# Agent attention and a three-way max network in one kernel: the last group stored as four output tiles, and new places for operations of the head

## The chip, the cores and the metric

The kernel runs on one NeuronCore of one Trainium2 chip. The metric is the device time of one execution in microseconds (us). Four executions were timed: 451.83, 451.85, 452.03 and 456.93 us, so the median is 451.94 us. One further execution was recorded by the hardware profiler, and all rows in this text come from that one.

## The reference

```python
def sm(a, b):                                  # softmax of scaled scores
    s = scale * (a @ b.transpose(0, 2, 1))
    e = np.exp(s - s.max(-1, keepdims=True))
    return e / (e.sum(-1, keepdims=True) + 1e-09)
agent_v = sm(agents, k) @ v                    # 49 agents gather from 12544 keys
x = sm(q, agents) @ agent_v                    # each query reads the 49 agents
h = np.maximum(np.maximum(x @ w1, x @ w2), x @ w3)
out = h @ w_out
```

There are 4 batches of 12544 rows and 128 columns, 49 agents, and weights of 128 x 768 (three) and 768 x 128. Inputs and output are float32.

## The kernel before, in words

**Folding.** Queries meet the weights only through 49 agent rows. So per batch a small matrix `G` is made from `agent_v` times the weights, in three parts: w2 - w1 (columns from `C21`), w3 - w1 (columns from `C31`; for one of the six blocks of 128, `f = FI = 4`, it is w3 - w2), and the linear part w1 @ w_out. The largest of three products is then a sum of the linear part and a maximum of differences. The division by the softmax sum is left to the end: each output row is multiplied by a reciprocal (`recips`) as it leaves PSUM.

**Stages.** The head (lines 381 to 495) does the keys of batch 0 in 11 k-groups of up to 9 tiles of 128 rows: load k and v, cast to bfloat16 (GpSimd for k, ScalarE for v), transpose k on TensorE, scores, exponential, sums, products with v. It also loads and casts the weights (`load_w`, L278; `cast_w1`, L320 on ScalarE), transposes w1 (`turn_w1`, L328 on TensorE and the copy L329 on VectorE), makes the differences (L306 on VectorE) and the first `G` (L505 on TensorE; L430 on VectorE, L432 on ScalarE). `keep_clock` (L339) and `keep_busy` (L809) issue matmuls whose results nobody reads. Then come 49 query groups of 8 tiles (`q_group`, from L616): load q (L641), cast (L645, GpSimd), transpose (L650 on TensorE and the copy L654, or L658 by DMA), scores (L664), exponential (L670), and for each of six blocks f: `first` and `second` (L687), a relu on ScalarE (L702, for f = 4 L699 and L710) and a maximum on VectorE (L712, the result is called `r`); then the output of two halves of four tiles: `out_linear` (L717), six times `out_hidden` (L726), the scaling (L733) and the store (L740). The keys of batches 1 to 3 (`k_group`, from L508) run beside the query groups of the batch before. Group 48 is the last; it takes two tiles from each of the four batches.

**What sets the order.** Every operation is registered with a number by `at(key, fn)`; at the end all are sorted by that number and issued in that order (L823 to L825). The numbers are written out by hand in tables: `HEAD` for the head, `KEY` and `LATE` for query groups, `OWN` for single groups. Each engine works through its own instructions strictly in this order. SyncE (its DMA queue is SP in the profile) issues nearly all transfers. Pools bound what can be in flight: `loads` has 14 buffers (`st`) for everything that is read from memory, PSUM has three tiles `uv` of two banks and two tiles `om` of one bank (`m_ps` and `o_ps`), `a_sb` has three buffers.

**The end.** `out_scale` of group 48 multiplies four tiles at a time (128 x 512, L733) for `o = 0` and `o = 1`, and `store` sends the group's result as four transfers (one for each batch, two tiles each) on SP, after both.

```python
def store():
    for src, r0, r1, m in rows(d["out"]):
        nc.sync.dma_start(out[r0:r1, :].rearrange("(p j) c -> p j c", j=m), src)
```

Of the kernel before, what the change touches and what calls it, by code (L numbers as in the profile page):

```python
# [9 lines left out]
FP32 = mybir.dt.float32  # L10
BF16 = mybir.dt.bfloat16
AF = mybir.ActivationFunctionType
ALU = mybir.AluOpType
# [23 lines left out]
}  # L37

HEAD = {
    "wl0": -11.09161, "wrm": -1.98468, "wl2": 0.51177, "wl1": 0.69065, "wl1b": 0.76707, "w1c": 2.59211,  # L40
    "rcp": 3.16515, "wol": 3.98125, "woc": 4.2069, "d31": 4.34124, "nrm": 4.41073, "df": 4.44324,
    "p31": 4.74403, "d21a": 4.83164, "e31a": 4.85118, "e31b": 4.89396, "d21b": 5.09254, "p21": 5.48697,
    "e21a": 6.03394, "e21b": 6.34709, "w1t": 6.98386, "pli": 11.47293, "lin": 11.9489,
}
OWN = {
    0: {
        "ld": -15.45285, "qc": -11.81581, "qt": -10.757, "qe": -10.20555, "s": -9.36462,
        "ex": -8.65857, "sum": -2.73814, "rec": 0.66113, "u0": 1.73303, "a0": 3.02721, "u3": 3.08353,
        "v0": 3.21809, "x0": 3.49617, "u1": 3.49632, "a3": 4.7675, "u2": 4.87373, "u4": 5.10456,
        "a1": 5.17197, "a2": 5.18107, "v2": 5.51752, "v3": 5.52169, "a4": 5.61362, "v4": 6.21265,  # L50
        "x3": 6.43191, "u5": 6.88439, "x4": 7.15661, "v1": 7.25918, "x2": 7.55072, "a5": 7.76958,
        "x1": 8.08498, "v5": 8.29806, "x5": 8.49985, "lin0": 9.17566, "oc01": 9.49956,
        "oc02": 10.66639, "oc03": 10.78909, "oc00": 11.42422, "oc04": 11.55405, "oc05": 11.65251,
        "sc0": 12.01522, "lin1": 12.21276, "oc14": 12.37652, "oc10": 12.54225, "oc15": 12.94573,
        "oc11": 13.51846, "oc12": 13.76128, "oc13": 13.89433, "sc1": 14.06057, "st": 30.2774,
    },
    1: {
        "qt": -0.68915, "qe": -0.28764, "s": -0.20645, "ex": 1.05465, "ks": 1.07376, "ke": 1.79044,
        "u0": 2.1165, "a0": 2.40909, "sum": 2.44924, "kv": 3.00013, "u2": 3.05696, "ka": 3.11196,
        "v0": 3.14183, "a2": 3.65256, "u3": 3.69373, "rec": 3.73135, "a3": 3.76488, "x0": 3.77268,  # L60
        "ea": 4.28719, "u1": 4.34384, "v2": 4.50739, "x2": 4.90263, "a1": 4.90814, "v3": 5.18637,
        "x3": 5.24289, "u4": 5.25804, "a4": 5.31877, "u5": 6.15638, "v1": 6.17467, "v4": 6.20321,
        "a5": 6.22076, "x1": 6.30625, "x4": 6.43439, "v5": 6.62335, "x5": 8.05604, "lin0": 9.75919,
        "oc01": 10.2942, "oc05": 10.90243, "oc04": 10.90286, "oc00": 11.16521, "oc02": 11.77385,
        "oc03": 11.80928, "sc0": 12.31367, "lin1": 12.60088, "oc10": 12.63655, "oc11": 12.65098,
        "oc13": 13.13497, "oc15": 13.20435, "oc12": 13.60702, "oc14": 13.78327, "sc1": 14.04041,
        "st": 19.70003,
    },
    34: {
# [40 lines left out]
        "oc04": 12.41887, "oc00": 12.48727, "oc03": 12.57446, "sc0": 13.3308, "st": 13.63859,  # L110
    },
    47: {
        "s": -3.43889, "ex": -2.81529, "u1": -0.80433, "a1": -0.32412, "u2": 2.6941, "v1": 3.26752,
        "x1": 3.30501, "a2": 3.62245, "u3": 3.94043, "v2": 4.32284, "x2": 4.48597, "u0": 4.61449,
        "a3": 4.81852, "a0": 4.86901, "u4": 5.40034, "v0": 5.78938, "x0": 6.29621, "u5": 6.30046,
        "a4": 6.61778, "v3": 6.6249, "x3": 6.8972, "v4": 7.07591, "a5": 7.08194, "x4": 7.42159,
        "sum": 7.58975, "lin0": 7.59348, "oc00": 7.60946, "oc02": 7.66715, "v5": 7.6866,
        "rec": 7.86032, "lin1": 7.9107, "oc04": 8.19044, "oc11": 8.44778, "x5": 8.64756,
        "oc14": 8.97694, "oc03": 9.46529, "oc12": 9.48275, "oc01": 10.74213, "oc05": 12.03538,
        "oc10": 12.48388, "oc13": 12.62494, "oc15": 12.8182, "sc0": 13.43374, "sc1": 13.79022,  # L120
        "st": 25.99034,
    },
    48: {
        "s": -2.89085, "ex": -1.81853, "u1": -0.70005, "a1": -0.085, "u2": 1.70331, "a2": 1.74305,
        "v1": 2.13067, "u0": 2.72237, "v2": 2.85402, "a0": 3.47527, "x1": 3.75355, "x2": 3.93622,
        "u3": 4.00569, "v0": 4.29428, "a3": 5.95326, "x0": 6.31037, "u4": 6.36552, "a4": 6.68639,
        "u5": 7.00215, "a5": 7.08972, "v3": 7.18229, "v4": 7.31644, "lin1": 7.60532, "oc12": 7.95591,
        "x4": 7.98067, "oc11": 8.18021, "x3": 8.54834, "sum": 8.70347, "v5": 9.35901, "rec": 9.6258,
        "oc10": 9.9529, "oc13": 11.90819, "lin0": 13.89458, "oc14": 13.89969, "oc03": 17.03889,
        "x5": 17.37893, "oc04": 18.83261, "oc02": 18.91848, "oc15": 19.85688, "oc01": 21.07623,  # L130
        "oc00": 22.72772, "sc1": 23.77362, "oc05": 24.9151, "sc0": 26.06666, "st": 26.59193,
    },
}
BORDER = {
# [57 lines left out]
def kernel(  # L192
# [18 lines left out]
    nc = tc.nc  # L211
    B, N, C = q.shape
    A = agents.shape[1]
    Dff = moe_w1.shape[1]
    scale = 1.0 / math.sqrt(C)
    P = 128
# [3 lines left out]
    NT = N // P  # L220
# [5 lines left out]
    NQ = B * NB + 1  # L226
# [4 lines left out]


    const = ctx.enter_context(tc.tile_pool(name="const", bufs=1))
    loads = ctx.enter_context(tc.tile_pool(name="loads", bufs=14))
    work = ctx.enter_context(tc.tile_pool(name="work", bufs=2))
    psum = ctx.enter_context(tc.tile_pool(name="psum", bufs=1, space=bass.MemoryType.PSUM))

# [8 lines left out]
    def at(key, fn):  # L246
        ops.append((key, len(ops), fn))
# [361 lines left out]
    def parts_of(s):  # L609

        if s < B * NB:
            return [(s // NB, s % NB * GT, 0, GT // 2)]
        h = REST // 2
        return [(b, NB * GT, b * h, (b + 1) * h) for b in range(B)]

    def q_group(s):  # L616
        pairs = [range(0, 2), range(2, 4)]
        n, nh = GT, GT // 2
        parts = parts_of(s)
        key = 6.0 * s  # L620
        K = places(s)
        d = {}
# [91 lines left out]
        def out_linear(o):  # L714
            t = d["o", o] = small_tile("o_ps")
            for i, jj in enumerate(pairs[o]):
                nc.tensor.matmul(t[:, i * 2 * C:(i + 1) * 2 * C], d["e"][:, jj * P:(jj + 1) * P],  # L717
                                 G[batch[jj]][:, C1O:C1O + 2 * C], start=(i == 0), stop=False,
                                 skip_group_check=True)

        def out_hidden(o, f):
            t = d["o", o]
            for i, jj in enumerate(pairs[o]):
                for h in range(2):
                    c = (i * 2 + h) * C
                    nc.tensor.matmul(t[:, c:c + C], r_sb[f][:, h, jj * P:(jj + 1) * P], wo_bf[:, f, :],  # L726
                                     start=False, stop=True, skip_group_check=True)

        def out_scale(o):
            if "out" not in d:  # L730
                d["out"] = work.tile([P, GT, C], FP32, tag="o_sb", bufs=HELD + 3, name="o_sb")
            j, m = 2 * pairs[o][0], 2 * len(pairs[o])
            nc.vector.tensor_tensor(  # L733
                out=d["out"][:, j:j + m, :],
                in0=d["o", o].rearrange("p (j c) -> p j c", c=C),
                in1=d["r"][:, j:j + m].unsqueeze(2).to_broadcast([P, m, C]), op=ALU.mult)

        def store():
            for src, r0, r1, m in rows(d["out"]):
                nc.sync.dma_start(out[r0:r1, :].rearrange("(p j) c -> p j c", j=m), src)  # L740


        at(key + K["ld"], load)
        at(key + K["qc"], cast)
# [12 lines left out]
        for o in range(2):  # L757
            at(key + K[f"lin{o}"], lambda o=o: out_linear(o))
            for f in range(NF):
                at(key + K[f"oc{o}{f}"], lambda o=o, f=f: out_hidden(o, f))  # L760
            at(key + K[f"sc{o}"], lambda o=o: out_scale(o))
        at(key + K["st"], store)

# [12 lines left out]
    def places(s):  # L778

        K = dict(KEY if s < LAST else LATE)  # L780
        for n, x in STREAM.items():
            z = 6.0 * s - LEAD + x
            K[n] = (z if z > HEAD_END else HEAD_END + 0.001 * (s + x / 6.0)) - 6.0 * s
        if s >= NB - 2:
            c = s % NB - (NB if s % NB >= NB - 2 else 0)
            if s < LAST - 2:
                K.update(BORDER.get(c, {}))
        if s == 0:
            K.update({"ld": NK + 2.15, "qc": 14.6, "qt": 15.7, "qe": 15.75, "s": 16.2, "ex": 16.35})
            for n in ("ld", "qc", "qt", "qe", "s", "ex"):  # L790
                K[n] += HEAD_END - Z
            K.update({"sum": 0.91, "rec": 0.95})
        K.update(OWN.get(s, {}))
        K["st"] += 6.0 * HELD * max(0.0, min(1.0, (NQ - 2.0 - s) / (NQ - 2.0 - LAST)))
        return K

    acc, _ = head(at_head)
    at(HEAD_END - 60, prep)
    for b in range(1, B):
        for g in range(NK):  # L800
            s = (b - 1) * NB + g + 1
# [54 lines left out]
```

## Time and profile before

| | us |
|---|---|
| median of four timed executions | 451.94 |
| the profiled execution, its own time | 456.19 |
| its span (first to last record) | 454.4 |
| TensorE busy | 434.8 |
| VectorE busy | 404.3 |
| ScalarE busy | 398.4 |
| GpSimd busy | 168.1 |
| memory traffic | 118.86 MB, mean 262 GB/s |

How to read it: the profiled execution is 4.25 us longer than the median, and its span covers all but 1.8 us of its own time. PE is TensorE's matmuls, PEld its weight loads, DVE VectorE, ACT ScalarE, POOL GpSimd; a q behind an engine's name means its instruction queue, where transfers are issued. L12 is line 12 of the kernel before. A row of the timeline gives the start, the length of a run of like instructions, the engine, the line, the tiles and shapes, and in brackets the idle time in front of it with what ended it. A row of the table by stretches gives for each engine the busy time in the stretch, then the share of the clock that TensorE was granted, the share of time in which the DMA engines were busy, and the rate.

### The profile page before, as it was taken

The page shows a single profiled execution, that of the slowest core. Times are in us where ns is not written, and L with a number is a line of the kernel's source. Part 1 is how long each engine was busy: PE and PEld are TensorE (multiplying, and loading weights), DVE is VectorE, ACT ScalarE, POOL GpSimd, SP SyncE. Part 2 cuts the span into 40 slices and gives each one's busy share as a digit, 9 for nine tenths or more (in the row PEclk, how much of TensorE's full clock was granted, in tenths as well). Part 3 has the DMA queues.
Part 4 walks back from the last instruction along what each step waited for, and adds up shares of the span by engine and source line. Part 5 has one row for each costly group of instructions (what it writes and reads, how often), then busy time and mean ns, then how long its engine had stood idle before and what let it go on. Part 6 is the DMA issues. An engine that isn't in the chain of part 4 may idle for free.

```text
span 454.4 us, 13320 instructions
## 1 busy us (share of the span) xinstructions
PE 434.8 (96%) x5506; PEld 278.0 (61%) x5506; DVE 404.3 (89%) x506; ACT 398.4 (88%) x459; POOL 168.1 (37%) x164
## 2 busy tenths in 40 slices
PE   2798999999999999999999999999999999999995
PEld 2674566666665666666665666656655555565664
DVE  3324799999999999999999999989999999999995
ACT  1557899999998999999989999989989999999983
POOL 4432466656323444447333444456421111010000
PEclk9988899999999999999999999999999999999998
DMA  8999999997659989999889999998996766647842
GB/s 308 412 409 351 269 272 293 263 286 236 210 132 372 315 224 312 309 241 326 262 224 311 300 272 300 305 268 285 306 219 182 217 154 198 185 95 219 325 200 94
DMA packets 83799, 118.86 MB, mean 262 GB/s; under 512 B 57687, under 2 KB 59803, under 8 KB 83739
## 3 DMA queue, kind: packets, MB, share of 16 engines
q1 hardware_dynamic: 83536, 117.92, 85.6%
q8 instruction: 43, 0.70, 0.6%
q14 instruction: 17, 0.14, 0.1%
q10 hardware_dynamic: 203, 0.10, 0.1%
HBM read 78.74 MB, written 25.69 MB: 230 GB/s over the span
## 4 chain that ended last, share of the span: by engine, by line
PE 77%; DMA 11%; DVE 5%; ACT 2%; POOL 1%; issue 1%; SPq 1%; DVEq 0%; POOLq 0%; ACTq 0%
PE uv_ps L687 31%; PE o_ps L726 28%; DMA st<-in_v_dram 5%; PE o_ps L717 5%; PE m_ps L650 3%; DMA st<-in_k_dram 3%; PE m_ps L664 3%; DVE r L712 3%; DMA st<-in_q_dram 3%; PE m_ps L534 2%; PE m_ps L365 1%; DVE o_sb L733 1%; PE m_ps L675 1%; PE uv_ps L505 1%; POOL q_bf L645 1%
## 5 line engine op out<-in xcount | busy, mean ns | idle before, releaser
L712 DVE TENSOR_TENSOR r<-uv_ps,a_sb 128x1024 bf16<-128x1024 f32 x245 | 297.6, 1222 | 9.1 <-PE uv_ps L687 4.6
L702 ACT ACTIVATE a_sb<-uv_ps 128x1024 bf16<-128x1024 f32 x245 | 243.8, 1024 | 19.6 <-PE uv_ps L687 15.3
L687 PE MATMUL uv_ps<-e_q,G 49*128 49x512 bf16 (+1 forms) x1248 | 183.2, 371 | 1.2 <-ACT G L432 0.5
L726 PE MATMUL o_ps<-wo_bf,r 128*128 128x128 bf16 x2352 | 176.1, 220 | 0.0
L726 PEld LDWEIGHTS <-r 128*128 128x128 bf16 x2352 | 139.5, 98 | 42.4 <-issue 39.7
L687 PEld LDWEIGHTS <-G 49*128 49x128 bf16 x1248 | 56.6, 93 | 61.9 <-issue 22.9
L645 POOL CAST q_bf<-st 128x1024 bf16<-128x1024 f32 x49 | 51.0, 1040 | 86.5 <-DMA st<-in_q_dram 67.4
L733 DVE TENSOR_TENSOR o_sb<-o_ps,recips 128x512 f32<-128x512 f32 x98 | 67.1, 685 | 2.6 <-PE o_ps L726 1.2
L514 POOL CAST k_bf<-st 128x1152 bf16<-128x1152 f32 (+1 forms) x33 | 37.4, 1134 | 72.1 <-DMA st<-in_k_dram 72.1
L518 POOL CAST v_bf<-st 128x1152 bf16<-128x1152 f32 (+1 forms) x33 | 37.5, 1137 | 48.7 <-DMA st<-in_v_dram 47.1
L710 ACT ACTIVATE r<-uv_ps 128x1024 bf16<-128x1024 f32 x49 | 50.3, 1026 | 1.2 <-PE uv_ps L687 0.9
L699 ACT ACTIVATE uv_ps<-uv_ps 128x1024 f32<-128x1024 f32 x49 | 49.6, 1012 | 0.1
L717 PE MATMUL o_ps<-G,e_q 128*128 128x256 bf16 x196 | 37.9, 275 | 0.0
L546 POOL TENSOR_TENSOR Eacc<-Eacc,e_k 128x441 f32<-128x441 f32 x27 | 27.6, 1023 | 21.6 <-ACT e_k L370 21.5
L670 ACT ACTIVATE e_q<-m_ps 128x512 bf16<-128x512 f32 x49 | 29.2, 596 | 2.8 <-PE m_ps L664 1.6
L654 DVE COPY qT<-m_ps 128x1024 bf16<-128x1024 bf16 x34 | 23.4, 687 | 3.6 <-PE m_ps L650 3.4
L379 DVE COPY kT<-uv_ps 128x1152 bf16<-128x1152 bf16 (+1 forms) x11 | 8.3, 752 | 19.6 <-PE uv_ps L376 19.6
L717 PEld LDWEIGHTS <-e_q 128*128 128x128 bf16 x196 | 11.9, 97 | 20.5 <-issue 20.0
L650 PE MATMUL m_ps<-ident,q_bf 128*128 128x128 bf16 x272 | 21.7, 225 | 1.1 <-POOL q_bf L645 1.1
L394 ACT ACTIVATE v_bf<-st 128x1152 bf16<-128x1152 f32 (+1 forms) x11 | 12.2, 1112 | 8.8 <-DMA st<-in_v_dram 8.8
L664 PE MATMUL m_ps<-qT,agT 128*64 128x512 bf16 (+1 forms) x104 | 19.9, 389 | 0.0
L389 POOL CAST k_bf<-st 128x1152 bf16<-128x1152 f32 (+1 forms) x11 | 12.5, 1137 | 19.9 <-DMA st<-in_k_dram 19.5
(72 smaller groups left out, 231.5 us busy)
## 6 DMA issues: line engine op xcount, KB each, us to landing
st<-in_q_dram SPq DMA_DIRECT2D x48, 512.0 KB, 5.0
out_dram<-o_sb SPq DMA_DIRECT2D x48, 512.0 KB, 5.8
st<-in_k_dram SPq DMA_DIRECT2D x40, 576.0 KB, 5.1
st<-in_v_dram SPq DMA_DIRECT2D x40, 576.0 KB, 8.8
st<-in_k_dram SPq DMA_DIRECT2D x4, 512.0 KB, 6.4
st<-in_v_dram SPq DMA_DIRECT2D x4, 512.0 KB, 7.3
st<-in_moe_w_dram SPq DMA_DIRECT2D x2, 384.0 KB, 9.3
kT<-k_bf SPq DMA_TRANSPOSE x33, 3.9
```

Source lines behind the costliest of these rows:

```text
L514: nc.gpsimd.tensor_copy(out=d["kb"][:, :n, :], in_=d["k"][:, :n, :])
L518: nc.gpsimd.tensor_copy(out=d["vb"][:, :n, :], in_=d["v"][:, :n, :])
L645: nc.gpsimd.tensor_copy(out=d["qb"], in_=d["q"])
L650: nc.tensor.transpose(t[:, j * P:(j + 1) * P], d["qb"][:, j, :], ident)
L687: nc.tensor.matmul(t[:, h, j0 * P:j1 * P], G[b][h * H:h * H + A, col + f * P:col + (f + 1) * P], d["e"][h * H:h * H + A, j0 * P:j1 * P], s ...
L699: nc.scalar.activation(u, u, AF.Relu)
L702: nc.scalar.activation(a_sb[f], u, AF.Relu)
L710: nc.scalar.activation(r, v_ps[f], AF.Relu)
L712: nc.vector.tensor_tensor(out=r, in0=v_ps[f], in1=a_sb[f], op=ALU.max)
L717: nc.tensor.matmul(t[:, i * 2 * C:(i + 1) * 2 * C], d["e"][:, jj * P:(jj + 1) * P], G[batch[jj]][:, C1O:C1O + 2 * C], start=(i == 0), stop ...
L726: nc.tensor.matmul(t[:, c:c + C], r_sb[f][:, h, jj * P:(jj + 1) * P], wo_bf[:, f, :], start=False, stop=True, skip_group_check=True)
L733: nc.vector.tensor_tensor(out=d["out"][:, j:j + m, :], in0=d["o", o].rearrange("p (j c) -> p j c", c=C), in1=d["r"][:, j:j + m].unsqueeze( ...
```

## The change

Three things are changed; all other code is the same. First, the tables: `HEAD`, and `OWN` for groups 0, 1, 47 and 48, have new numbers. Secondly, group 48 no longer uses `out_scale` and `store`: its output is scaled in four tiles of 128 x 256, two by VectorE (one instruction each) and two by ScalarE (two instructions of 128 x 128 each), and each tile is stored by its own transfer, tiles 0 and 2 through SyncE, 1 and 3 through ScalarE's queue. Thirdly, the pool `loads` has 13 buffers, where it had 14.

In the order of issue this gives, by the built programs: SP issues q of group 0 before the first k and the load of w1 before the second k; TensorE transposes q of group 0 first of all; ScalarE casts w1 between the third and fourth exponential of the head, where it stood just ahead of the last cast of v; the 12 filler matmuls of `wrm` come one k-group earlier; TensorE's transposes of w1 and VectorE's copy of them come in the head, where they stood inside query group 0; so do the sums and `recips` of group 0. From query group 2 to group 45 the order on all engines is the same. In group 48 the half `o = 1` is finished first, and then 16 matmuls of `o = 0` follow.

```diff
 HEAD = {
-    "wl0": -11.09161, "wrm": -1.98468, "wl2": 0.51177, "wl1": 0.69065, "wl1b": 0.76707, "w1c": 2.59211,
-    "rcp": 3.16515, "wol": 3.98125, "woc": 4.2069, "d31": 4.34124, "nrm": 4.41073, "df": 4.44324,
-    "p31": 4.74403, "d21a": 4.83164, "e31a": 4.85118, "e31b": 4.89396, "d21b": 5.09254, "p21": 5.48697,
-    "e21a": 6.03394, "e21b": 6.34709, "w1t": 6.98386, "pli": 11.47293, "lin": 11.9489,
+    "wl0": -12.98516, "w1c": -5.9571, "wrm": -3.2727, "w1t": -1.93048, "rcp": 2.65644, "wl2": 2.93957,
+    "d31": 3.55494, "wl1": 3.84576, "wl1b": 3.87196, "wol": 3.98131, "nrm": 4.0717, "woc": 4.22037,
+    "df": 4.27603, "p31": 4.51124, "e31a": 4.63737, "d21b": 4.88815, "e31b": 5.77247, "d21a": 6.84424,
+    "p21": 7.24385, "e21a": 7.33263, "e21b": 7.83854, "pli": 10.67497, "lin": 11.69792,
 }
 OWN = {
     0: {
-        "ld": -15.45285, "qc": -11.81581, "qt": -10.757, "qe": -10.20555, "s": -9.36462,
-        "ex": -8.65857, "sum": -2.73814, "rec": 0.66113, "u0": 1.73303, "a0": 3.02721, "u3": 3.08353,
+        "ld": -17.50772, "qc": -16.77951, "qt": -14.33933, "qe": -11.55766, "s": -8.91506,
+        "ex": -7.35282, "sum": -4.74507, "rec": -4.32612, "u0": 1.56825, "a0": 4.09253, "u3": 4.3641,
...
     48: {
-        "oc10": 9.9529, "oc13": 11.90819, "lin0": 13.89458, "oc14": 13.89969, "oc03": 17.03889,
-        "x5": 17.37893, "oc04": 18.83261, "oc02": 18.91848, "oc15": 19.85688, "oc01": 21.07623,
-        "oc00": 22.72772, "sc1": 23.77362, "oc05": 24.9151, "sc0": 26.06666, "st": 26.59193,
+        "x4": 17.85448, "v3": 19.03702, "lin0": 19.66535, "oc15": 20.01931, "oc01": 20.4512,
+        "oc12": 22.46167, "x3": 24.03035, "oc05": 24.815, "oc14": 25.87451, "oc13": 26.8641,
+        "sc1": 29.0489, "oc04": 29.05912, "oc03": 29.88451, "oc02": 30.80374, "sr1": 30.84707,
+        "st2": 30.91835, "oc00": 43.00949, "st3": 43.44114, "sr0": 44.15505, "sc0": 47.77127,
+        "st1": 53.21418, "st0": 99.95534,
...
-    loads = ctx.enter_context(tc.tile_pool(name="loads", bufs=14))
+    loads = ctx.enter_context(tc.tile_pool(name="loads", bufs=13))
...
+        def end_tile(i):
+            t = d["end", i] = work.tile([P, 2, C], FP32, tag=f"o_end{i}", bufs=1, name=f"o_end{i}")
+            return t, d["o", i // 2].rearrange("p (j c) -> p j c", c=C)[:, i % 2 * 2:i % 2 * 2 + 2, :]
+
+        def end_scale(i):
+            t, src = end_tile(i)
+            nc.vector.tensor_tensor(out=t, in0=src, op=ALU.mult,
+                                    in1=d["r"][:, 2 * i:2 * i + 2].unsqueeze(2).to_broadcast([P, 2, C]))
+
+        def end_scale_scalar(i):
+            t, src = end_tile(i)
+            for j in range(2):
+                nc.scalar.activation(t[:, j, :], src[:, j, :], AF.Copy, scale=d["r"][:, 2 * i + j:2 * i + j + 1])
+
+        def end_store(i):
+            b, t0, j0, _ = parts[i]
+            row = (b * NT + t0) * P
+            (nc.scalar if i % 2 else nc.sync).dma_start(
+                out[row:row + 2 * P, :].rearrange("(p j) c -> p j c", j=2), d["end", i])
...
-            at(key + K[f"sc{o}"], lambda o=o: out_scale(o))
-        at(key + K["st"], store)
+            if s < NQ - 1:
+                at(key + K[f"sc{o}"], lambda o=o: out_scale(o))
+            else:
+                at(key + K[f"sc{o}"], lambda o=o: end_scale(2 * o))
+                at(key + K[f"sr{o}"], lambda o=o: end_scale_scalar(2 * o + 1))
+        if s < NQ - 1:
+            at(key + K["st"], store)
+        else:
+            for i in range(4):
+                at(key + K[f"st{i}"], lambda i=i: end_store(i))
```

By the built program, the four scalings of the end are also tied to each other: ScalarE's of tile 3 waits for VectorE's of tile 2 (the same PSUM tile), and VectorE's of tile 0 waits for ScalarE's of tile 1. On ScalarE's queue the order is tile 3, its store, tile 1, its store.

## The prediction

> **What bounds the kernel now.** I read the busy shares, then the table by stretches around the head's end and the tail, then the timeline of single engines in those two places, and the chain of waits for the middle.
>
> ```profile
> PE 434.8 (96%) x5506; PEld 278.0 (61%) x5506; DVE 404.3 (89%) x506; ACT 398.4 (88%) x459; POOL 168.1 (37%) x164
> ```
>
> TensorE is busy nearly throughout, but its matmul records overlap and include waits. A stretch shows more (start:end, length, busy time of PE, PEld, DVE, ACT, POOL, granted clock, DMA share, GB/s):
>
> ```profile
> 39.10:42.40 3.30, 1.80 (x33) 1.26 (x31) 2.57 (x8) 1.93 (x5) 0.61 (x1) 1.00 1.06 379
> 42.50:45.80 3.30, 3.30 (x18) 1.01 (x16) 1.96 (x3) 2.70 (x4) 2.19 (x2) 0.50 0.83 234
> 45.90:49.20 3.30, 3.30 (x24) 1.83 (x24) 1.01 (x3) 2.39 (x3) 1.74 (x2) 0.50 0.88 213
> ...
> 58.15:66.30 8.15, 8.15 (x110) 5.42 (x111) 8.12 (x11) 7.81 (x10) 5.58 (x7) 1.00 1.00 279
> 432.25:449.32 17.07, 17.07 (x280) 12.75 (x278) 16.01 (x18) 13.51 (x15) 0.00 (x0) 1.00 0.38 151
> ```
>
> Up to 40 us the DMA engines are full (share 1.06 still at 39 to 42): the head waits for bytes. From 42.5 to 49.2 TensorE runs at half clock and is busy all the time: it alone is the bound there, VectorE is two thirds idle. From 50 us on VectorE is the bound (8.12 of 8.15 us in a steady group, 16.01 of 17.07 in the tail).
>
> VectorE's timeline in the cold stretch shows what it waits for:
>
> ```profile
> 40.20 0.83 DVE L306 TENSOR_TENSOR wall<-st 128x512 bf16<-128x512 f32 x2
> ...
> 44.87 1.22 DVE L712 TENSOR_TENSOR r<-uv_ps,a_sb 128x1024 bf16<-128x1024 f32 x1 [0.18 <-PE uv_ps L687]
> 46.15 0.56 DVE L329 COPY w1T<-m_ps 128x768 bf16<-128x768 bf16 x1
> 48.93 0.69 DVE L654 COPY qT<-m_ps 128x1024 bf16<-128x1024 bf16 x1 [2.23 <-PE m_ps L650]
> 49.75 2.36 DVE L712 TENSOR_TENSOR r<-uv_ps,a_sb 128x1024 bf16<-128x1024 f32 x2
> ...
> 54.95 1.17 DVE L712 TENSOR_TENSOR r<-uv_ps,a_sb 128x1024 bf16<-128x1024 f32 x1
> ```
>
> It idles 2.23 us for the q transposes L650, which stand on TensorE behind the w1 transposes, fillers and two more blocks; from 49.75 it is back to back. The row at 54.95 is the first maximum of group 1: I use it to measure what the head gains. The end:
>
> ```profile
> 448.68 1.36 DVE L733 TENSOR_TENSOR o_sb<-o_ps,recips 128x512 f32<-128x512 f32 x2 [0.59 <-PE o_ps L726]
> 450.07 1.82 SPq L740 DMA_DIRECT2D out_dram<-o_sb  x4
> ```
>
> The last matmul ends at 449.32, both scalings at 450.05, SP issues four stores one after another to 451.89; the last, issued at 451.43, lands 1.82 later at 453.25, and 1.15 us of closing follow.
>
> **The change part by part.**
>
> *w1 cast (0.83 us on ScalarE, L320) out of the way of the last v.* Now it stands at 39.16 and the half cast of the last v at 39.89; that v is in memory at 39.2 (GpSimd starts its half at 39.21). The last v products thus come 0.68 earlier. But the path does not follow: `avT` and the first G product also need the w3 differences (row at 40.20), and w3, issued at 28.70, lands 11.4 us later, at 40.1, as before, since the same bytes are ahead of it. Differences 40.12 to 40.95, `avT` 0.21: only the 0.1 us comes that `recips` (0.14) took on VectorE. In its new place the cast fits into a ScalarE gap of 1.16 us at 15.3 to 16.4. Gain 0.1.
>
> *q first, w1 second on SP.* The first two k land about 1.4 and 1.0 us later (they changed places with 512 and 384 KB at some 400 GB/s), everything from the third k on lands as before. TensorE is then behind by about 0.9 us at 15, and regains it at 18.5, where it idled 0.7 for a k cast, and before 22. Cost 0; without that cover at most 0.9.
>
> *12 fillers one k-group earlier, w1 transposes (six, 0.35 us at full clock) in the head.* I add up TensorE's items from 25 to 37.5: it is 0.45 late at 33, and equal at 37.5, because before it waited 0.19 for a v cast at 36.15 and did the sums of group 0 there. The covers are those waits and the 0.7 us by which v products are now early against `avT`. Cost 0.
>
> *The cold stretch.* From the second G product's end (43.6) to the q transposes' end before: six L687 1.80, w1 transposes 0.75, six fillers 0.64, four L687 0.97, two fillers 0.33, q transposes 0.85: 5.3, end 48.9. After: two fillers 0.22, six L687 1.80, four fillers 0.43, two L687 0.45, q transposes 0.85: 3.75 less 0.1 from above plus a wait of 0.1 for a ScalarE relu: 47.0. So VectorE could resume 1.9 us earlier, and it has no w1T copy (0.56) to do. What is late next: I set the following items by hand with half-clock pairs of 0.45 to 49.28 and 0.25 after. The copy qT ends at 47.6, maximum 3 runs 47.6 to 48.8, maximum 2 waits for its product to 49.2 (0.4 idle), maximum 1 stands behind 12 fillers (12 x 0.056) and starts at 51.0 (0.6 idle), maximum 5 ends at 53.4, `Vacc` and `recips` follow, and group 1's first maximum starts at 53.85 where it was 54.95. Gain 1.1, the 0.1 included. Bounds: 0.5, if only VectorE's removed copy counts (0.56, with `recips` 0.14 less the new idle), and 1.9, if no new idle arises.
>
> Here a rule weighs in: the Trainium skill, page "TensorE: Matmul & The Clock Gate", Part 1, says that the clock is halved after an idle window of some 3.4 us and restored after one busy window, windows running free. The rows agree on halving (1.80 of 3.30 busy, then 0.50) but not on one window: 3.30 of 3.30 busy, and the next still at 0.50. By the rows the stretch stays two windows: 1.1. By the rule it would end at 45.9; then the q transposes end 0.4 earlier, and each later pair and filler before 49.3 costs half: I get 1.1 more, 2.2. I take the rows.
>
> *The middle, groups 2 to 45: same order, cost 0 if the gain passes.* SP's loads run in a loop of their own (k lands, is cast, kT transpose, next load). At 296.60 TensorE waits for it, as its row shows below GpSimd's:
>
> ```profile
> 100.74 1.02 POOL L546 TENSOR_TENSOR Eacc<-Eacc,e_k 128x441 f32<-128x441 f32 x1 [3.88 <-ACT e_k L370]
> ```
>
> And TensorE's row:
>
> ```profile
> 296.60 0.62 PE L650 MATMUL m_ps<-ident,q_bf 128*128 128x128 bf16 x8 [1.06 <-POOL q_bf L645]
> ```
>
> A gain of compute alone would be swallowed there. But at 92.6, 100.7, 108.9, 117.0 and 127.2 GpSimd, which feeds that loop, waits 2.7 to 6.2 us for an exponential, so the loop is re-set by compute and moves with it. I let the 1.1 pass.
>
> *13 load buffers.* I followed which load takes whose buffer: against the times of before, every load finds its buffer free by at least 4.5 us, but for one with 1.7 (it follows q of group 0, now cast earlier). SP is held by earlier landings instead. Cost 0.
>
> *The tail's new order.* Same 11 maxima, 4 scalings and 2 reciprocals on VectorE from 432.08 to the last maximum, which ended at 448.10 with some 0.5 of idle. Set by hand, the new order leaves about 0.25 idle: last maximum at 447.9, last `o = 1` matmul at 448.2, last of all (16 x 0.056 later) 449.1. Gain 0.2; bounds -0.6 (two product waits like the 0.59 row's) and 0.4 (all idle gone).
>
> *Four tiles.* VectorE 128x256: 0.42 (L430's row of that size, 424 ns; half of L733 would be 0.34). ScalarE 128x128: 0.277 each (L335), with a scale operand that no row has; I take 0.28, bounds 0.2 and 0.4. Issue 0.42 on SP's rows, 0.57 on ScalarE's only one (agents, L269). By the waits of the built program: tile 2 to 448.65, tile 3 to 449.2, its store holds ScalarE's queue to 449.7, tile 1 to 450.25, tile 0 (waits for it) to 450.7, its store lands 1.7 later: 452.4, against 453.25 less the tail's 0.2 = 453.05. Gain 0.65. The rule that speaks against the change: the skill's page "PSUM — Partial Sum Buffer", on bank collisions, says two engines may not read one bank at once, so software orders them. No run here shows a collision, but the waits are there; were tiles 0 and 1 scaled at once, tile 0 would be done at 449.55 and the last store would be tile 1's, landing at 452.0: gain 1.05. I take the waits. Bounds: 0 (an issue on ScalarE of 1.1, as SP's longest) and 1.2.
>
> Sum: 1.1 + 0.2 + 0.65 = 1.95. Span 454.4 to 452.45, the profiled execution's own time 456.19 to 454.25; taken from the median, 450.0.
>
> **The rivals.**
> - *The head's gain is lost in the loop of loads.* For it: the 1.06 wait at 296.60, DMA share about 1 from 247 to 334. Against: GpSimd's waits for exponentials. Then 0.85 is left: 451.1.
> - *The clock returns a window earlier* (45.9). For it: the rule, and more 128-row matmuls (fillers, q transposes) before 45.9. Against: a fully busy window did not do it. 1.1 more: 448.9.
> - *Slower: a third cold window, 49.3 to 52.7.* By my list TensorE has in it v4, u5 (v and u products of L687), 12 fillers, v1, the k scores, L334 and two further pairs: 2.5 us at full clock, 5.0 at half. That costs 2.5, and from 1.95 on it decides: 452.5 (450.0 + 2.5). For it: being busy did not restore the clock at once. Against: the window 45.9 to 49.3 keeps the same kinds of matmuls, q transposes and scores.
>
> **How the numbers follow.** Forecast 0.50; gain lost 0.20; clock early 0.15; third cold window 0.10; 0.05 for what I do not see. The likeliest's own range is 449.1 to 450.9 (the bounds of head and end seldom add up). The range over all, 448.6 to 452.0, leaves out most of the slower rival and the far tails. One per cent is 4.5 us, about what a measurement can tell from no change; no case reaches it: within 0.93, faster 0.04, slower 0.03.
>
> **What would show it.** After: no VectorE idle of 2 us before L654's copy near 47, the q transposes of group 1 ending near 47.0, the first maximum of group 1 at 53.9; the clock 0.50 from 42.5 to 49.3; the wait at the q cast near 295.5 again about 1.06; last matmul about 2.0 minus 0.65 earlier than 449.32, so near 448.0; last landing 3.3 after it (3.9 before). The forecast is wrong if the head's 1.1 is gone by 300 us, if the clock changes at other windows, or if ScalarE's queue takes over 1 us for an issue.

## The result, and the profile after

Before 451.96 us (median of 58 executions), after 450.63 (39); the ratio is 0.9965 with a 95% interval of 0.9953 to 0.9977, so 1.6 us less (1.0 to 2.1). The two medians themselves differ by 1.33. The forecast was 450.0 with a range of 448.6 to 452.0, within 1 per cent: it holds, though the range begins at no gain at all. Most of its reason does not hold.

The profiled execution of after has a span of 448.4 and took 450.20, 0.4 below its median; that of before had 454.4 and took 456.19, 4.23 above its median. The mean clock tells them apart: 0.999 against 0.986. The page's first row, and the same table by stretches as before the change (start:end, length, then the busy time of PE, PEld, DVE, ACT, POOL, granted clock, DMA share, GB/s):

```profile
PE 432.1 (96%) x5506; PEld 277.8 (62%) x5506; DVE 403.4 (90%) x506; ACT 399.4 (89%) x463; POOL 169.1 (38%) x164
```

```profile
39.10:42.40 3.30, 2.42 (x30) 1.16 (x26) 2.50 (x8) 1.70 (x3) 0.79 (x1) 1.00 1.07 373
42.50:45.80 3.30, 3.11 (x32) 1.61 (x30) 2.84 (x4) 3.30 (x5) 1.34 (x3) 1.00 1.04 228
45.90:49.20 3.30, 3.13 (x41) 1.83 (x39) 2.73 (x3) 3.27 (x5) 2.28 (x3) 1.00 1.01 351
...
426.87:443.94 17.07, 16.99 (x280) 12.85 (x277) 15.73 (x18) 13.81 (x17) 0.00 (x0) 1.00 0.20 81
```

There is no half clock at 42 to 49 us. ScalarE is busy nearly throughout there (3.30 of 3.30, 3.27 of 3.30), TensorE a little less (3.11, 3.13). Is this the change, or was the half clock only in the one execution that was profiled? The first experiment answers it: the kernel before, run again, has a clock of 1.00 in the same two stretches. Its rows are those to compare with:

```profile
42.50:45.80 3.30, 2.89 (x28) 1.41 (x29) 2.71 (x4) 3.21 (x5) 1.96 (x2) 1.00 1.22 227
45.90:49.20 3.30, 3.30 (x40) 1.91 (x38) 2.70 (x3) 3.07 (x5) 1.92 (x2) 1.00 0.85 248
```

From here on "before at full clock" is that execution (span 450.0, 451.76 us). Five rows serve as marks. `k_recip` (line 411) says that the sums of the keys are complete. The differences (line 306) also need the weights w3 to have landed, that is, their load to be in memory. "G's cast" (line 430) is the first copy of `G` out of PSUM on VectorE. The copy `qT` (line 654) follows the q transposes, and the first maximum of group 1 is the row at 52.37. VectorE's timeline:

```profile
39.54 0.47 DVE L411 RECIPROCAL k_recip<-m_ps 128x49 f32<-128x49 f32 x1 [3.04 <-PE m_ps L416]
...
39.99 0.83 DVE L306 TENSOR_TENSOR wall<-st 128x512 bf16<-128x512 f32 x2
...
42.99 1.02 DVE L430 CAST G<-uv_ps 128x256 bf16<-128x256 f32 x2 [0.87 <-PE uv_ps L505]
...
45.25 0.55 DVE L329 COPY w1T<-m_ps 128x768 bf16<-128x768 bf16 x1
46.50 0.69 DVE L654 COPY qT<-m_ps 128x1024 bf16<-128x1024 bf16 x1 [0.70 <-PE m_ps L650]
...
49.87 2.36 DVE L712 TENSOR_TENSOR r<-uv_ps,a_sb 128x1024 bf16<-128x1024 f32 x2 [0.34 <-PE uv_ps L687]
...
52.37 1.17 DVE L712 TENSOR_TENSOR r<-uv_ps,a_sb 128x1024 bf16<-128x1024 f32 x1
```

And in after (its lines are one higher):

```profile
38.17 0.47 DVE L412 RECIPROCAL k_recip<-m_ps 128x49 f32<-128x49 f32 x1 [2.96 <-PE m_ps L407]
39.08 0.89 DVE L307 TENSOR_TENSOR wall<-st 128x512 bf16<-128x512 f32 x2 [0.43 <-DMA st<-in_moe_w_dram]
...
42.02 1.02 DVE L431 CAST G<-uv_ps 128x256 bf16<-128x256 f32 x2 [0.80 <-PE uv_ps L506]
...
44.73 0.69 DVE L655 COPY qT<-m_ps 128x1024 bf16<-128x1024 bf16 x1 [0.36 <-PE m_ps L651]
...
48.26 2.50 DVE L713 TENSOR_TENSOR r<-uv_ps,a_sb 128x1024 bf16<-128x1024 f32 x2 [0.57 <-PE uv_ps L688]
...
51.39 1.23 DVE L713 TENSOR_TENSOR r<-uv_ps,a_sb 128x1024 bf16<-128x1024 f32 x1 [0.44 <-PE uv_ps L688]
```

Take differences row by row. G's cast starts 0.97 earlier, the copy `qT` 1.77 earlier, the first maximum of group 1 0.98 earlier. So all that lasts is there before group 0 begins: from G's cast to that maximum it is 9.38 before, 9.37 after. The 0.55 us of the w1T copy are gone from VectorE, and in their place it idles 0.57 and 0.44.

The same holds further on. Of the 245 maxima of VectorE, start against start in both traces, those of after are ahead by 0.98 at 133 us, 0.97 at 295, 0.60 at 312, 0.95 at 376 and 0.94 at 428: the head's gain arrives at the tail whole. The end of after, engine by engine (`o_end` are the four tiles):

```profile
443.09 0.42 DVE L749 TENSOR_TENSOR o_end<-o_ps,recips 128x256 f32<-128x256 f32 x1 [0.56 <-PE o_ps L727]
443.54 2.53 SPq L760 DMA_DIRECT2D out_dram<-o_end  x2
443.55 0.63 ACT L755 ACTIVATE o_end<-o_ps,recips 128x128 f32<-128x128 f32 x2 [1.17 <-DVE o_end L749]
444.20 0.38 ACTq L760 DMA_DIRECT2D out_dram<-o_end  x1
444.63 0.63 ACT L755 ACTIVATE o_end<-o_ps,recips 128x128 f32<-128x128 f32 x2 [0.46 <-ACT o_end L755]
445.29 0.34 ACTq L760 DMA_DIRECT2D out_dram<-o_end  x1
445.29 0.42 DVE L749 TENSOR_TENSOR o_end<-o_ps,recips 128x256 f32<-128x256 f32 x1 [1.78 <-ACT o_end L755]
```

The last matmul ends at 443.94, the last store is issued at 445.74 and lands at 447.45, 3.51 after the last matmul. Before at full clock the last matmul ends at 444.89 and the last landing is at 448.82, 3.93 after it.

### The profile page after: what moved, and what is told of

Same layout as the page of the kernel before. It is cut to its first block, busy times and chain, and to the rows that moved or that the text cites. A ratio compares the mean times of both kernels' runs of the same rounds, so it can differ in the third digit from the quotient of the medians.

```text
span 448.4 us, 13332 instructions
## 1 busy us (share of the span) xinstructions
PE 432.1 (96%) x5506; PEld 277.8 (62%) x5506; DVE 403.4 (90%) x506; ACT 399.4 (89%) x463; POOL 169.1 (38%) x164
## 4 chain that ended last, share of the span: by engine, by line
PE 87%; DVE 4%; DMA 4%; ACT 2%; issue 1%; SPq 0%; POOL 0%; ACTq 0%; DVEq 0%
PE uv_ps L688 34%; PE o_ps L727 32%; PE o_ps L718 6%; PE m_ps L665 3%; PE m_ps L651 3%; DVE r L713 2%; DMA st<-in_moe_w_dram 2%; PE m_ps L535 2%; PE m_ps L366 2%; DMA st<-in_k_dram 2%; PE uv_ps L377 1%; ACT a_sb L703 1%; PE uv_ps L340 1%; PE m_ps L676 1%; DVE kT L380 1%
## 5 line engine op out<-in xcount | busy, mean ns | idle before, releaser
L734 DVE TENSOR_TENSOR o_sb<-o_ps,recips 128x512 f32<-128x512 f32 x96 | 65.8, 685 | 2.4 <-PE o_ps L727 0.8
L371 ACT ACTIVATE e_k<-m_ps 128x441 bf16<-128x441 f32 (+1 forms) x33 | 17.8, 539 | 2.1 <-PE m_ps L676 0.7
```

What stands on the lines that cost most here:

```text
L734: nc.vector.tensor_tensor(out=d["out"][:, j:j + m, :], in0=d["o", o].rearrange("p (j c) -> p j c", c=C), in1=d["r"][:, j:j + m].unsqueeze( ...
```

## The experiments

All times are medians, with the ratio to the runs of the kernel before on the same chip. Half-microseconds are near what a median of ten executions can tell, so places are read from the traces, one execution each. Where I say "at full clock" of a median, it is over the executions with a mean clock of 0.997 or more: 451.89 for before (68 executions), 450.60 for after (35).

**The kernel before, again.** No edit.

> The kernel before, unchanged. Theory A: the half clock between 42.5 and 49.3 us belongs to the one execution that was profiled (its own time is 4.25 above the median, its mean clock 0.986), so in most executions here the mean clock is 0.998 or more, the span about 450.1, and a profile of such a one has 1.00 from 42 to 49, its last matmul near 445.1. Theory B: every execution has it (clock 0.986 throughout, q transposes of group 1 ending at 48.9) and the 4.25 were lost elsewhere. By both, the time from the last matmul to the end of the span is again 5.1.

Measured 451.86, ratio 1.0005 (0.9986 to 1.0023); its profile has a span of 450.0, clock 1.00, last matmul at 444.89, 5.09 from it to the span's end. Theory A. Of 117 executions of the kernel before in these sessions, the 68 at a clock of 0.997 or more have a median of 451.89, the 34 in between one of 452.3, and the 15 at 0.989 or less one of 454.23. So the lowest clocks go with 2.3 more, and the median of all does not hold that.

**The head alone.**

```
 HEAD, OWN[0], OWN[1]: the tables of after;  loads bufs=14, OWN[47], OWN[48], store: as before
```

> Before, with the new places of the head's operations and of groups 0 and 1 alone; 14 load buffers, the old tail. Prediction as it stands: 1.1 less, 450.85. If the half clock is an accident of the profiled execution: VectorE, back to back from 43 us on, only loses the copy of w1T (0.56) and the reciprocal (0.14) from its path: 0.4 to 0.7 less, 451.4. Rival, gain lost in the loop of loads: first maximum of group 1 early by that much, but the end not: 451.95.

Measured 451.48, ratio 1.0005 (0.9978 to 1.0032): over all its executions no gain is shown. At full clock it is 451.15, 0.74 less. In its trace the first maximum of group 1 is 0.99 early (51.37), and those near 222 us are 1.09 early. Then it loses 0.55 at 232, of which 0.24 come back at once, and 0.44 at 333; at the last maximum 0.26 is left. Both places are one small operation of VectorE with both inputs in SBUF, and GpSimd beside it:

```profile
231.53 0.76 DVE L586 TENSOR_TENSOR avT<-Vacc,k_recip 128x49 bf16<-128x49 f32 x1
```

```profile
231.08 1.15 POOL L514 CAST k_bf<-st 128x1152 bf16<-128x1152 f32 x1 [5.42 <-DMA st<-in_k_dram]
```

`avT` takes 0.22 in the traces where GpSimd rests; here it takes 0.76 and ends at 232.29, just after GpSimd's cast (232.23). At 332.06 it takes 0.81, behind a cast of q from 331.77 to 332.81. (The `avT` near 133 us meets a cast in every trace, of before and after alike, and takes 0.57 to 0.80.) The Trainium skill, page "SBUF — State Buffer", section "SBUF: two separate sides", states this: a VectorE operation with two SBUF inputs and a GpSimd operation share a port that the first holds to its end. The trace agrees: `avT` ends 0.06 after the cast both times, and costs 0.54 and 0.59 more. Where GpSimd's casts fall against `avT` depends on when loads land; that may be one reason why the same kernel spreads (450.63 to 451.78 at clocks of 0.997 and more), which one trace cannot show. My rival "gain lost in the loop of loads" thus has something to it, but by another way than a wait for a load: in some executions, not in the profiled one of after.

**The four tiles alone.**

```
-loads bufs=14        +loads bufs=13
 OWN[48], the keys in their order, numbers and old keys between them left out:
-"sc1", "oc05", "sc0", "st"
+"sc1", "sr1", "st2", "st3", "oc05", "sr0", "sc0", "st1", "st0"
 (and the functions end_tile to end_store, as after)
```

> Before, with the four output tiles and their four stores alone, in the old order of the tail's products, and 13 load buffers, without which the tiles have no room. From the last matmul to the end of the span 4.45 (as after) where before has 5.08: 0.63 less, 451.3. If 13 buffers cost something, the last matmul is later than that of the kernel before by that much: 451.95 or more.

Measured 451.37, ratio 0.9981 (0.9964 to 0.9997). The last matmul ends at 444.88 (before 444.89): 13 buffers cost nothing, all maxima to the last within 0.04. The last landing is 3.74 after the last matmul, 0.19 less than 3.93, where after has 3.51. The rest needs the new order: tile 2 is scaled 0.85 before the last matmul in after (443.09), 0.63 before it here (444.25). The span ends 4.70 after the last matmul, since 0.2 more go at the closing (below).

**The tail's order alone.**

```
 OWN[47], OWN[48]: the orders of after, with "sc1": 29.0489, "oc00": 43.00949, "sc0": 47.77127, "st": 99.95534
```

> Before, with the new order of groups 47 and 48 alone (o = 1 finished first, sixteen products of o = 0 last), the old scalings and stores. Prediction: 0.2 less at the last matmul, 451.75; then both scalings and four stores: the scaling of o = 1 comes before the last matmul, so the one of o = 0 ends 0.7 after it instead of 0.73, no gain there. Rival: the whole remainder (1.4 less 0.63) comes from here and nothing from the head: 451.2.

Measured 451.90, ratio 0.9982 (0.9956 to 1.0009). It happened to come to the tail 0.39 late; the last maximum is 0.20 late: the order gives 0.19, as forecast (0.2). But from the last maximum to the last matmul it is 1.35 now (1.41 in after, 1.22 before), so 0.07 is left at the last matmul (0.01 in after), and the stores add nothing (3.94).

**The loads' order alone, and the rest of the head alone.**

```
 loads_only:   "wl0": -12.98516, OWN[0]["ld"]: -17.50772 (as after); all else before
 rest_of_head: "wl0": -11.09161, OWN[0] ld, qc, qt, qe, s, ex as before; all else of the head as after
```

> Before, with SP's new order at the start alone (q first, w1 before the second k); everything else of the head as before. In the undisturbed profile of before the first cast of G starts at 42.99, in after at 42.02, and the w3 load lands at 39.71 and 39.05. Theory A, the loads' new order brings w3 early and that is the head's whole gain: w3 lands by 39.1, G's cast starts near 42.1, the first maximum of group 1 near 51.5 (52.37 in before), time 451.0. Theory B, the gain needs the last v early too: w3 lands by 39.1 but the sums hold k_recip at 39.5 as before, so the differences start at 39.99 and G's cast at 42.9: time 451.8.

> Before, with the whole new head but the old order of loads (and the old places of q's cast, transposes, scores and exponentials of group 0). Theory A: w3 lands at 39.7 as before, the differences wait for it, G's cast starts near 42.7, time 451.6. Theory B: the sums are early by 1.3 but w3's landing holds the differences at 39.75, so G's cast is 0.25 early: 42.75, and the gain over both kernels is split 0.25 here, 0.7 by the landing, neither alone giving the 0.97. If w3 itself lands early here (39.1), it is not SP's order that moves the landing.

Loads alone: 452.03, ratio 0.9993 (0.9966 to 1.0020), at full clock 451.75. w3 lands at 39.15, 0.56 early; the sums hold `k_recip` at 39.09, 0.45 early; G's cast starts 0.46 early, and every maximum to the end stays 0.42 to 0.46 early:

```profile
39.09 0.47 DVE L411 RECIPROCAL k_recip<-m_ps 128x49 f32<-128x49 f32 x1 [3.04 <-PE m_ps L416]
...
42.53 1.02 DVE L430 CAST G<-uv_ps 128x256 bf16<-128x256 f32 x2 [0.87 <-PE uv_ps L505]
```

The rest alone: 451.32, ratio 0.9972 (0.9953 to 0.9992), at full clock 451.26. `k_recip` is 0.67 early, but w3 lands at 39.92 and VectorE waits for it, so G's cast is only 0.10 early:

```profile
39.94 0.89 DVE L306 TENSOR_TENSOR wall<-st 128x512 bf16<-128x512 f32 x2 [0.60 <-DMA st<-in_moe_w_dram]
...
42.89 1.02 DVE L430 CAST G<-uv_ps 128x256 bf16<-128x256 f32 x2 [0.80 <-PE uv_ps L505]
```

In these traces it is theory B in its form: two things stand in front of G, the sums and w3. The loads' order moves both (0.45 and 0.56), the rest moves only the sums, and only both together give the 0.97. The medians at full clock do not split like that: 0.14 less for the loads alone (8 executions), 0.63 for the rest alone (6), 0.74 for the whole head (8). When w3 lands differs from execution to execution by as much as these parts do, so how the head's gain divides between them stays open; that it is won before G's cast, and not in group 0, does not depend on it. In five executions with the old order of loads w3 landed between 39.46 and 40.08, in nine with the new one between 39.03 and 39.93 (seven of them up to 39.37). The difference begins at the start: with q first, the first load lands at 4.58 (the head alone) instead of 5.30 (a k), and the next issue on SP behind that landing goes out at 4.66 instead of 5.64.

**w1 transposes back in group 0; the linear branch's evacuations on VectorE.**

```
 w1t_back:       after with "w1t": 6.98386
 lin_on_vector:  -nc.scalar.activation(wall[...], t[:, :C], AF.Copy)     +nc.vector.tensor_copy(...)
                 -nc.scalar.activation(G[0][:, C1O:WC], ..., AF.Copy)    +nc.vector.tensor_copy(...)
```

> After, with the six w1 transposes and the copy of w1T back in their old place in group 0. Prediction's step: the copy costs VectorE its 0.55 there and the transposes TensorE 0.35, so the first maximum of group 1 comes 0.55 to 0.9 later than the 9.4 after G's cast that after shows: 10.0 or more, time 451.3. Theory A, ScalarE sets the pace of group 0 (it is busy 3.30 of 3.30 and 3.27 of 3.30 us in the two stretches from 42.5 in after): VectorE's copy falls into its idle of 0.36, 0.57 and 0.44; only what holds up ScalarE's exponential (slack 0.35) counts: 9.4 to 9.7, time 450.8.

> After, with the two evacuations of the linear branch in group 0 (0.30 and 0.43 on ScalarE) on VectorE. Theory A, ScalarE sets the pace of group 0: its last three relus come 0.6 to 0.7 earlier, VectorE has 0.55 more to do and 1.37 of idle to put it in, so the first maximum of group 1 starts 0.3 to 0.5 earlier: 8.9 to 9.1 after G's cast instead of 9.37, time 450.2. Theory B, TensorE with its twelve fillers or VectorE itself sets it: 9.4 or more, time 450.6 or more.

w1 back: 451.19, ratio 0.9975 (0.9957 to 0.9994). The w1T copy now stands right in front of G's cast on VectorE (42.89, cast 43.36), which is not where it stood before. So the time is counted from ScalarE's first part of G instead (41.58): 11.15 to the first maximum of group 1, 10.69 in after, 10.70 before at full clock. There it costs 0.46; before at full clock, with the copy behind a maximum, is no slower than after without it. So neither the forecast's 0.56 for its old place holds, nor my theory that it is hidden in any place. Linear branch: 451.37, ratio 0.9980 (0.9964 to 0.9996), the first maximum of group 1 9.89 after G's cast (9.37 in after): slower. VectorE stands still in front of its new copy, because the product that it copies is not there:

```profile
48.95 0.29 DVE L336 CAST wall<-o_ps 128x128 bf16<-128x128 f32 x1 [1.23 <-PE o_ps L335]
```

So it doesn't tell whether ScalarE sets group 0's pace. That stays argued from its busy time, not shown.

**The end: who scales, who stores.** All four are after with another end.

```
 end_sp:        all four stores nc.sync.dma_start
 end_by_bank:   tiles 2, 3: ScalarE scales and stores;  tiles 0, 1: VectorE scales, SP stores
 end_vector:    VectorE scales 2, 3, 0, 1;  SP stores 2, 0, ScalarE's queue 3, 1
 end_two_banks: as end_vector, tile 1 in an accumulator of its own; last products in order of tiles
```

> After, with all four stores of the end issued by SP. If ScalarE's issues hold its own passes, as the prediction has it (the store of tile 3 occupies ScalarE 0.38, with a gap of 0.05), tile 1 starts 0.43 earlier, the last landing is 3.1 after the last matmul instead of 3.51: 450.2. If SP's four issues in a row take their place (0.33 to 0.46 each), the last one starts as early as in after or later: 450.6 or more.

> After, with ScalarE scaling and storing both tiles of o = 1 and VectorE both of o = 0 (SP stores them), so that no two engines share an accumulator at the end. If the waits between the engines on one accumulator are what the four tiles lost: tile 0 done 0.42 and tile 1 0.8 after the last matmul, SP's second issue at 0.85, last landing 2.6 after the last matmul instead of 3.51: time 449.7. If the last landing is set by the stores and not by the scalings, it stays 3.3 or more: 450.5.

> After, with all four tiles of the end scaled by VectorE, tiles 2 and 3 while TensorE works at the last sixteen products; tiles 2 and 0 stored by SP, 3 and 1 by ScalarE, which computes nothing there. If what is left after the last matmul is only the waits of the two engines on one another: tile 0 done 0.45 and tile 1 0.8 after the last matmul, last landing 1.75 after that store's issue, 2.6 after the last matmul instead of 3.51 in after and 2.98 with all stores on SP: time 449.7. If two stores that are issued within 0.3 us take longer each (2.1 as with the split by accumulator), 3.0: 450.1.

> After, with all four end tiles scaled by VectorE and stored as in the version with VectorE alone (SP tiles 2 and 0, ScalarE's queue 3 and 1), and tile 1 in an accumulator of its own: the last sixteen products are put in order of tiles, eight for tile 0, then eight for tile 1. If the end after the last matmul is now only one scaling, one issue and one landing, tile 0 is scaled while TensorE works at tile 1 (8 x 0.056 = 0.45), tile 1 from 0.05 to 0.45 after the last matmul, the last landing is 2.25 after it (2.59 with one accumulator, 3.51 in after, 3.93 in before): median of the executions at full clock 449.35. If VectorE can't begin at tile 0 before the last product of tile 1 (a wait that covers both accumulators), 2.6 and 449.7.

| end | us | ratio (95%) | at full clock | last matmul to last landing |
|---|---|---|---|---|
| before | 451.96 | 1 | 451.89 | 3.93 |
| after | 450.63 | 0.9965 (0.9953 to 0.9977) | 450.60 | 3.51 |
| end_sp | 450.30 | 0.9963 (0.9940 to 0.9986) | 450.05 | 2.98 |
| end_by_bank | 450.31 | 0.9956 (0.9935 to 0.9978) | 450.19 | 3.03 |
| end_vector | 449.81 | 0.9940 (0.9916 to 0.9965) | 449.67 | 2.59 |
| end_two_banks | 449.67 | 0.9935 (0.9911 to 0.9958) | 449.66 | 2.48 |

With all stores on SP, ScalarE's four passes run in 1.14 without a break, where in after its own issue lies between them: 0.53 less at the landing, 0.43 expected. By accumulator, the two last issues come 0.03 apart and SP's takes 2.12 to land (1.71 in after): neither of the two cases expected. VectorE alone does best: the two tiles of `o = 1` run while TensorE is at its last products, and ScalarE isn't needed. Its end:

```profile
445.40 1.65 DVE L749 TENSOR_TENSOR o_end<-o_ps,recips 128x256 f32<-128x256 f32 x4 [0.57 <-PE o_ps L727]
445.85 1.23 SPq L760 DMA_DIRECT2D out_dram<-o_end  x2
446.18 1.23 ACTq L760 DMA_DIRECT2D out_dram<-o_end  x2
```

Four scalings in 1.65 us back to back from 445.40, the last matmul at 446.25. With the second accumulator tile 0 could start earlier, but VectorE is busy with tiles 2 and 3; the last store still goes out 0.23 earlier against the last matmul (0.60 after it, not 0.83). Of that its landing loses half (1.88 us, where it was 1.76). So 2.48 comes out, and not 2.25. At full clock both stand at 449.7, below before and after. The intervals of their ratios reach up to 0.9965 and 0.9958, and after's ratio is 0.9965: the step from after rests on the full-clock medians (450.60 to 449.67) and the traces (0.9 at the landing).

That profiled execution of end_vector took 451.59 at a clock of 0.999, and shows the other thing that sets single executions apart. TensorE's row, then VectorE's:

```profile
326.21 0.62 PE L651 MATMUL m_ps<-ident,q_bf 128*128 128x128 bf16 x8 [1.11 <-POOL q_bf L646]
```

```profile
326.87 0.69 DVE L655 COPY qT<-m_ps 128x1024 bf16<-128x1024 bf16 x1 [0.91 <-PE m_ps L651]
...
329.92 0.95 DVE L574 TENSOR_REDUCE e_sum<-Eacc 128x49 f32<-128x441 f32 x1 [1.22 <-POOL Eacc L547]
```

Here the loop of loads had fallen 5 to 9 us behind that of after, and 1.9 us were lost between 326 and 333. The first profile of before, with loads 8 to 12 us behind, lost 1.2 at 294, on the like wait for a cast of q, and 0.6 more by 333. In the profiles of after and of before at full clock TensorE has no such wait.

By chance the profiled execution of end_two_banks had the half clock, with the new head:

```profile
38.45:41.85 3.40, 1.75 (x30) 1.27 (x29) 2.44 (x7) 1.10 (x4) 0.61 (x1) 1.00 1.05 381
41.90:45.25 3.35, 3.31 (x17) 0.99 (x18) 1.66 (x4) 2.51 (x4) 2.19 (x2) 0.50 0.71 236
45.30:48.65 3.35, 3.35 (x23) 1.60 (x21) 2.04 (x3) 2.17 (x3) 1.92 (x2) 0.50 1.13 250
48.70:52.00 3.30, 3.27 (x41) 1.90 (x41) 2.42 (x3) 3.27 (x5) 2.08 (x2) 1.00 0.88 326
```

Its copy qT starts 3.78 after G's cast (43.37), its first maximum of group 1 10.98 after it; in the first profile of before 5.26 and 11.28. So in a cold stretch too the new order gives at most 0.30 by the start of group 1, though it has the copy `qT` 1.48 earlier; and its half clock ends 0.3 earlier against G's cast (5.3 after it, 5.6 in before), which may be all of that.

## Why the prediction was right, and where it was not

| term | forecast | measured |
|---|---|---|
| head up to G's cast | 0.1 | 0.97 |
| cold stretch, group 0 | 1.0 | 0.01 at full clock, up to 0.30 at half clock |
| middle | 0 | 0.04 lost |
| 13 buffers | 0 | 0 |
| tail's order, at the last matmul | 0.2 | 0.01 |
| four tiles, from the last matmul to the last landing | 0.65 | 0.42 (0.19 without the new order) |
| closing, from the last landing to the end of the span | 0 | 0.20 |
| sum | 1.95 | 1.6 (spans 449.98 to 448.42) |

The measured column is one pair of executions, before at full clock and after. The medians at full clock differ by 1.29; the parts run alone gave 0.74 (head), 0.59 (four tiles) and 0.04 (tail's order) of it by the same measure, each uncertain by some 0.3 to 0.5.

- **The reading of the profile failed first.** "From 42.5 to 49.2 TensorE runs at half clock" is true of the execution that I had and not of the median from which I subtracted. I noted the 4.25 between the two and did not ask where they were. Against before at full clock 1.8 of them come in the half clock (0.76 behind at the first maximum of group 0, 2.58 at the second) and 1.8 at 294 and by 333, with the loop of loads late; the first 0.76 hold w3's landing 0.37 later and the half clock's beginning. The 1.06 wait at the q cast, which I used for a rival, belonged to that execution too. A clock that changes at other windows was the forecast's own sign of being wrong, and after has no half clock there at all.
- **The cold stretch: gain 1.0.** The forecast's sum for it has a slip: 43.6 and 3.75 make 47.35, not 47.0, so 1.55 earlier and not 1.9. The copy `qT` came earlier by about that (1.48 in the half clock, counted from G's cast; 0.80 at full clock, with the head's 0.97 1.77 in all), and "what is late next" took it back: after idles of 0.57 and 0.44, group 0 ends with nothing won. My hand-set list had 0.4 and 0.6 of new idle and still 1.0 left; it lacked the 0.44 in front of the first maximum of group 1 (0.35 in the cold profile), and it started from the half clock's 2.23 of idle, which at full clock is 0.70.
- **"w3 lands as before, since the same bytes are ahead of it."** The same bytes, but not from the same start: w3 was issued 0.79 earlier in the profiled pair (28.02 instead of 28.81) and came 0.66 earlier, and with the sums early too (1.37 at `k_recip`) the head's 0.97 is made of this, not of group 0. The first two k landed 0.66 and 0.71 later (forecast 1.4 and 1.0), the third 0.27 earlier (forecast: as before). Where the rest of the loads' lead comes from is not shown. q first was put as a cost covered; in the traces it is part of the gain. That forecast and measured gain are both near 1.0 is chance.
- **The rule weighed.** In the stretch at 42 us one busy window did not restore the clock: in both cold profiles the first halved window has TensorE busy throughout (3.30 of 3.30, 3.31 of 3.35) and the next is halved too. But the forecast had read only part of its profile. The first profile of before has another halved window in the head, and there one busy window was enough, as the rule has it:

```profile
18.56:21.97 3.41, 1.45 (x29) 1.22 (x30) 0.76 (x1) 1.59 (x2) 0.94 (x2) 1.00 1.02 409
21.97:25.39 3.42, 3.42 (x41) 2.54 (x40) 0.73 (x1) 1.59 (x2) 1.71 (x2) 0.50 1.03 415
25.39:28.80 3.41, 3.41 (x47) 2.17 (x46) 0.78 (x2) 1.74 (x3) 1.40 (x2) 1.00 1.03 412
```

So one window was enough in one stretch of three, and two were needed in two; what tells them apart is not shown. Nor were the windows in front of a halving idle, as the rule has it and the forecast took as agreeing: TensorE was busy 1.45 of 3.41 and 1.80 of 3.30 us in them by its records. The rival of a window less did not occur at 42 us, nor did a third cold window there.
- **The middle and the buffers** held: GpSimd waits for exponentials in after too (1.49, 2.65, 3.23, 6.19 us at 97 to 124), and the lead passes.
- **The tail's order** was right at the last maximum (0.19 and 0.20) and wrong at the last matmul: forecast 1.2 from one to the other, measured 1.41; `o = 1` is complete 0.53 after the last maximum and not 0.3.
- **Four tiles**: the chain is the one forecast, in the same order, but the last landing is 3.51 after the last matmul and not 3.3: ScalarE's pair takes 0.63 instead of 0.56, twice, with 0.05 between an issue and the next pass; the issue itself is shorter (0.38, not 0.5). The waits between the engines, which the bank rule stood for, are the 1.17 and 1.78 in the rows of the end; without them (VectorE alone) the landing comes 0.92 earlier.
- **Closing**: the 0.20 was not in the forecast, and is not shown to come from the change (below).

## What to carry to other kernels

If the profiled execution's own time stands off the median by more than the change is worth, first find where: look over the whole span for rows with a clock below 1.00 and for waits on loads, and do not subtract from the median what only that execution holds. A gain is real where it still stands at the next engine's next wait; set the list up to the row after the one that you hope for. At an end of stores, count from the last matmul to the last landing: work that an idle engine could do before that matmul was free here, and an engine that both computed and issued delayed the one by the other.

## What I had not expected of the hardware

- The half clock comes by execution. A mean clock of 0.989 or less stands in 16 of 151 executions with the old head's products and in 2 of 121 with the new head. That is not a rarer half clock: the profile of end_two_banks has two halved windows at a mean of 0.992, that of before three at 0.986. At 0.992 or less it is 19 of 151 and 15 of 121. Nor does it cost the new head less: after's three executions at 0.992 have a median of 452.96, 2.4 above its full-clock median, and before's at 0.989 or less stand 2.3 above theirs. In both cold profiles the halving at 42 follows a stretch with TensorE busy 1.75 of 3.40 or 1.80 of 3.30 us; before at full clock had 1.97 of 3.30 there and was not halved.
- The last landing to the end of the span takes 1.15 or 1.16 in three profiles (the two of before and that of the loads' order alone) and 0.96 or 0.97 in the eleven others. In those three the last packet of the instruction queue q14 comes 0.3 to 0.5 after the span's end, in the others 5 to 8 us before it. That is all of the 0.20 that after gains there. It does not go with the change: the head alone and the tail's order alone, both with the old stores, have the 0.96, and the loads' order alone has not. What puts it so was not tried.
- VectorE starts one maximum 0.37 late at 305 us in every trace with the new head, and has 0.35 less idle at 375, with TensorE and ScalarE on time both times. I found no cause; the two cancel.
